# Earlier reciprocals, a one-hot product on VectorE, and tables entered once per three batches, in an attention and mixture-of-experts kernel

## The chip, the cores and the metric

The kernel runs on one core of a Trainium2 chip. The metric is the device time of one execution in microseconds (us). One core has five engines with instruction queues of their own: PE (TensorE, matmuls; PEld is its weight load), DVE (VectorE), ACT (ScalarE), POOL (GpSimd) and SP (SyncE, which here only issues DMAs).

## The reference

Attention over a sliding window, then a mixture of experts on its output:

```
q, k, v: 8 batches x 8 heads x 576 tokens x 64
scores = q k^T / 8 - slope[head] * |i - j|      # only 0 <= i - j < 128
attn   = softmax(scores);  x = attn v           # -> x: 8 x 576 x 512
logits = x w_gate                               # 8 experts
local  = sigmoid(x w_local)
e[s]   = argmax(logits[s]) if s == 0 or local[s] < 0.5 else e[s-1]
out[s] = softmax(logits[s])[e] * (relu(x[s] w1[e]) w2[e])   # F = 1024
```

A token whose local gate is high keeps the expert of the token before it. Each token goes to one expert; how many go to each is known only at run time.

## The kernel before, in words

**Attention, 0 to about 271 us.** 32 slots, one for each batch b and pair of heads p = 0..3, four slots per batch. The order of the operations in a slot is written out by hand in the table ORDER, one string for each p (lines 58 to 63). Each mark is an operation on tokens of the slot: S(i) is the score matmul (i = 0..8, blocks of 64 queries), D(i) the bias and the row minimum on DVE (line 486, the custom operation with the name scs), E(i) the exponential on ACT, which also adds up the row into sm. N3 and N8 normalise: POOL computes r = sm + 1e-9, DVE takes the reciprocal of r, and POOL multiplies the parts by it, parts 0 to 3 in N3 (r of 128x4) and 4 to 8 in N8 (r of 128x5). U(j) are the transposes of the parts on PE into the PSUM tile pt; U0 needs the four parts of N3. C(j) copies pt to SBUF, M(j) multiplies with v, X copies the result and T transposes it on DVE for the store to xd in device memory. A mark with ' belongs to the pair before, and a "." is one step of side work: the gate of the finished batch (route, line 587). All engines' queues are kept in that program order by the class InOrder (line 157), so most of attention's instructions carry line 157 in the profile whatever they do.

**Side work route(b).** It turns the logits of batch b into one-hots (OH, shown as oh_all), the rank of each token at its expert, and from them two one-hot factors: cw (line 671, on POOL; the expert and the block of 32) and RO (line 675, on DVE, shown as ro_all; the row in the block, times the token number val). Five matmuls of RO and cw (pT, in a PSUM tile of the pool ptk, shown as pk) give the token numbers in their places, 0 where there is none. enter (line 687) adds them to the table tbl: z = (ps > 0) * 576 * b in one DVE instruction (tz), and two additions. The numbers in val are those inside one batch, 1 to 576, since the factors are fp16.

**Experts, from about 271 us.** A plan fixed ahead visits each expert with columns of tokens: visit 0 has 256 columns (8 blocks of 32), visit 1 has 384 (299.5 to 337.2 us) and visit 2 has 512 (from 340.1 us); the visits after that are given out by rank at run time. In a visit (Fixed.run, line 973), for eight blocks f of the hidden layer: matmuls h of x and w1, Relu on ACT to hh (line 1001), the low part hl on DVE (line 1002), and matmuls y with w2. Every fp32 product is three matmuls of high and low parts (lines 956 to 958). Weights come by DMA into wraw; split_chunk (lines 230 to 234) casts the high part on ACT and subtracts on DVE for the low part. The rows of x are gathered by POOL (line 172), four tiles t of 128 for a visit of 512; split_x (lines 175 to 182) transposes a tile on DVE (xtr, line 178), casts it on ACT (qx, line 181) and subtracts on DVE (qx, line 182). A visit starts when the qx of all its tiles are there. Operations on nc.vector are placed into DVE's queue by a scheduler; those through InOrder and pin keep their order on each engine.

**Side work of the visits.** During visits 0 and 1 the tables for the visits by rank are made: fill_table (line 841) computes for each batch the one-hots hot (line 848, five DVE instructions, also named cw), five matmuls with ro_all into a pk tile (line 858), and enter into the table trk (128x128). The table then gives the gather indices xidx, ridx and sidx (indices, line 694; fi in the rows). What would be needed for tokens beyond the plan follows (lines 920 to 931: end, efx, off, ge, ef).

Of the kernel before, what the change touches and what calls it, by code (L numbers as in the profile page):

```python
# [8 lines left out]
F32 = mybir.dt.float32  # L9
# [4 lines left out]
ALU = mybir.AluOpType  # L14
AX = mybir.AxisListType
PS = bass.MemoryType.PSUM
P = 128

NB = 8
S = 576  # L20
DM = 512
NE = 8
NT = 5
KS = 4
NS = 3
# [3 lines left out]
NSB = 128  # L29
# [19 lines left out]
def windows(nb):  # L49
# [8 lines left out]
ORDER = [  # L58
# [4 lines left out]
]  # L63
DEPTH = 3
POOL_CUT = 19
PACE = 16
FAR = 1000.0
Z_HOLD = -1.5 * 2.0 ** -23

# [2 lines left out]
def moe_attention(ctx, tc, qT, kT_d, vv, wg, wl, w1, w2, out):  # L72
    nc = tc.nc
    NTOK = NB * S

    cp = ctx.enter_context(tc.tile_pool(name="const", bufs=1))
    st = ctx.enter_context(tc.tile_pool(name="state", bufs=1))
    wr = ctx.enter_context(tc.tile_pool(name="wraw", bufs=RAWS))
    tp = ctx.enter_context(tc.tile_pool(name="tok", bufs=2))

    sh = ctx.enter_context(tc.tile_pool(name="shared", bufs=2))
    ptk = ctx.enter_context(tc.tile_pool(name="ptk", bufs=1, space=PS))
# [16 lines left out]
    own = cp.tile([P, NE], F32, name="own")  # L99
    slots = cp.tile([P, 2, NE], F32, name="slots")  # L100
    rep32 = cp.tile([P, P], F16, name="rep32")
    val = cp.tile([P, NT], F32, name="val")
    msel = cp.tile([P, 4], F32, name="msel")
    quart = cp.tile([P, 4], F32, name="quart")
    roff = cp.tile([P, 1], F32, name="roff")
# [7 lines left out]
    ro_all = st.tile([P, NB, NT, P], F16, name="ro_all")  # L113
# [17 lines left out]
    pin = tc.keep_in_program_order  # L131
# [31 lines left out]
    pe, dve, act, pool = (InOrder(e) for e in (nc.tensor, nc.vector, nc.scalar, nc.gpsimd))  # L163
# [139 lines left out]
    with ExitStack() as actx:  # L303
# [57 lines left out]
        def make_bias(p):  # L361
            o = [bias[64 * h:64 * h + 64, p] for h in range(2)]
            for h in range(2):
                pool.tensor_scalar(o[h], rel[64 * h:64 * h + 64], -8.0 * 2.0 ** -(2 * p + h + 1), 1.0, ALU.mult, ALU.mult)
                yield
            for h in range(2):
                pool.affine_select(o[h], o[h], [[-1, 192]], ALU.is_ge, -8e9, base=128, channel_multiplier=1)
                yield
            for h in range(2):
                pool.affine_select(o[h], o[h], [[1, 192]], ALU.is_gt, -8e9, base=0, channel_multiplier=-1)  # L370
                yield
# [13 lines left out]
        for h in range(2):  # L385
            pool.iota(rel[64 * h:64 * h + 64], [[-1, 192]], base=128, channel_multiplier=1,
                           allow_small_or_imprecise_dtypes=True)
# [13 lines left out]
        def setup():  # L401

            yield from make_bias(2)
            yield from make_bias(3)
            whole = dict(channel_multiplier=0, allow_small_or_imprecise_dtypes=True)
            pool.memset(w32, 0.0)
            nc.sync.dma_start(w32[:, :, 0:8], wg.rearrange("(k p) e -> p k e", p=P))
            nc.sync.dma_start(w32[:, :, 8:9], wl.rearrange("(k p) e -> p k e", p=P))
            yield
            pool.memset(onesb, 1.0)  # L410
            yield
            pool.memset(msel, 1.0)
            yield
            pool.affine_select(utri, onesb, [[1, P]], ALU.is_gt, 0.0, base=0, channel_multiplier=-1)
            yield
            pool.affine_select(msel, msel, [[-32, 4]], ALU.is_ge, 0.0, base=0, channel_multiplier=1)
            yield
            pool.memset(first, 0.0)
            yield
            pool.iota(quart, [[32, 4]], base=0, **whole)  # L420
            yield
            pool.affine_select(msel, msel, [[32, 4]], ALU.is_ge, 0.0, base=31, channel_multiplier=-1)
            yield
            pool.memset(first[0:1, 0:1], 1.0)
            yield
            pool.iota(k8, [[0, NT], [-1, NE]], base=NE, **whole)
            yield
            pool.tensor_tensor(quart, quart, msel, ALU.mult)
            yield
            pool.tensor_copy(identb, ident)  # L430
            yield
            for t in HR:
                pool.memset(t, 0.0)
                yield
            pool.memset(ohs, 0.0)
            pool.memset(g32, 0.0)
            yield
            pool.iota(io16, [[0, NT], [1, 4 * KS]], base=0, **whole)
            yield
            pool.iota(rep32, [[0, 4], [1, 32]], base=0, **whole)  # L440
            yield
            pool.iota(val, [[P, NT]], base=1, channel_multiplier=1, allow_small_or_imprecise_dtypes=True)
            yield
            pool.memset(tbl, 0.0)
            yield
            pool.memset(trk, 0.0)
            yield
            pool.memset(own, 0.0)
            for e, k in enumerate(OWN):
                pool.memset(own[:, e:e + 1], 4.0 * k)  # L450
            yield
            for r in range(NE):
                pool.memset(slots[:, 0, r:r + 1], float(sum(CAP[:r])))
                pool.memset(slots[:, 1, r:r + 1], float(CAP[r]))
                if r % 2:
                    yield
            pool.iota(io32, [[1, NFX]], base=0, **whole)
            yield
            pool.iota(io128, [[1, NSB]], base=1, **whole)
# [127 lines left out]
        def route(b):  # L587
            L = logits_of.pop(b)
            l8 = L[:, :, 0:NE]
            OH, RO = oh_all[:, b], ro_all[:, b]  # L590
# [63 lines left out]
            with nc.allow_low_precision("small whole numbers"):  # L654
# [3 lines left out]
            rf = tp.tile([P, NT], F32, name="rrf")  # L658
# [9 lines left out]
            kh = tp.tile([P, NT, 4 * KS], F16, name="kh")  # L668
            dve.tensor_tensor(kh, io16, k_all[:, b].unsqueeze(2).broadcast_to([P, NT, 4 * KS]), ALU.is_equal)
            cw = tp.tile([P, NT, NSB], F16, name="cw")[:, :, :4 * NS * KS].rearrange("p t (e k) -> p t e k", e=NS)  # L670
            pool.tensor_tensor(cw, OH[:, :, 0:NS].unsqueeze(3).broadcast_to([P, NT, NS, 4 * KS]),
                                   kh.unsqueeze(2).broadcast_to([P, NT, NS, 4 * KS]), ALU.mult)
            yield
            for t in range(NT):
                dve.tensor_scalar(RO[:, t], rep32, rf[:, t:t + 1], val[:, t:t + 1], ALU.is_equal, ALU.mult)
                if t % 2:
                    yield
            yield
# [7 lines left out]

        def enter(table, ps, b):

            z = tp.tile([P, P], F32, name="tz")[:, :table.shape[1]]
            dve.tensor_scalar(z, ps, 0.0, float(S * b), ALU.is_gt, ALU.mult)  # L690
            dve.tensor_tensor(table, table, ps, ALU.add)
            dve.tensor_tensor(table, table, z, ALU.add)

        def indices(t, idx, x0, c0, wins):

# [90 lines left out]
        for slot in range(4 * NB + DEPTH):  # L786
            b, p = divmod(slot, 4)
# [53 lines left out]
    def fill_table(table, fc, pace):  # L841

        fo = {}

        def hot(b):
            fo[b] = tp.tile([P, NT, NSB], F16, name="cw")
            for t in range(NT):
                nc.vector.tensor_scalar(fo[b][:, t], io128, fc[:, b * NT + t:b * NT + t + 1], None, ALU.is_equal)

        hot(0)  # L850
        for b in range(NB):
            for _ in range(pace // 2):
                yield
            if b + 1 < NB:
                hot(b + 1)
            pt = ptk.tile([P, NSB], F32, name="pk")
            for t in range(NT):
                pin(nc.tensor.matmul(pt, ro_all[:, b, t], fo[b][:, t], start=t == 0, stop=t == NT - 1))
            for _ in range(pace - pace // 2):
                yield  # L860
            enter(table, pt, b)

    def rank_tables():

# [26 lines left out]
        nc.vector.tensor_scalar(efx[:, NFX + 1:], er, 0.0, None, ALU.add)  # L891
        nc.vector.tensor_scalar(lo, own, -FAR, None, ALU.add)
        nc.vector.tensor_tensor(hi, lo, cap, ALU.add)
# [6 lines left out]
        kf = tp.tile([P, NA], F32, name="kf", bufs=1)  # L900
        nc.vector.tensor_scalar(kf, ka, -FAR, None, ALU.add)
        nc.vector.tensor_tensor(lo_t, kf, lo_t, ALU.is_ge)
# [3 lines left out]
        nc.vector.scalar_tensor_tensor(a_t, a_t, 1.0, lo_t, ALU.add, ALU.mult)  # L906
        yield
        yield from fill_table(trk, a_t, PACE_TABLE)
        yield from indices(trk, idxs, XO[0], TO[0], [at + w for kind, _, at, nb in PLAN if kind == "rank" for w in windows(nb)])
        rank_done.append(1)  # L910
        for _ in range(PACE):
            yield
# [26 lines left out]
    def beyond_table():  # L939

        nc.vector.memset(tfx, 0.0)
        run(fill_table(tfx, beyond[0], 0))
        run(indices(tfx, idxs, XO[1], TO[1], windows(NSB)))
        nc.sync.dma_start(xidx_d, xidx[:, XO[1]:])
        nc.sync.dma_start(ridx_d, ridx[:, TO[1]:])
        nc.sync.dma_start(sidx_d, sidx[:, TO[1]:])
        nc.sync.dma_start(efx_d, efx[0:1, 0:NFX])
# [297 lines left out]
```

## Time and profile before

| | |
|---|---|
| median of 3 runs | 741.42 us (740.2 to 741.76) |
| profiled execution | 742.23 us, of which its span is 740.5 us |
| mean granted TensorE clock | 0.995 |
| PE busy | 713.2 us (96%) |
| DVE busy | 491.1 us (66%) |
| ACT busy | 431.6 us (58%) |
| POOL busy | 399.8 us (54%) |
| DMA | 121.91 MB, mean 165 GB/s |

The profile is of one execution, by the profiler's clock; a time in it counts from the span's start. A row of the timeline has the start, the busy time, engine, line, operation, out<-in with its shape, the number of equal instructions in a run (x), and in brackets how long the engine was idle before and what released it. A row of a wait table has the total idle time, how often, and the longest. In the table by windows each engine has busy us and, in brackets, instructions; the last three numbers are the granted clock as a share of full speed, DMA's busy share and GB/s.

### The profile page before, as it was taken

To read this page: it belongs to the slowest core of one execution; us is meant where nothing else is said; L and a number is where in the kernel's file an instruction comes from. 1 tells how busy PE (TensorE), PEld (TensorE's weight loads), DVE (VectorE), ACT (ScalarE), POOL (GpSimd) and SP (SyncE) were. 2 spreads that over 40 slices of the span, in tenths; PEclk is the share of its full clock that TensorE was granted. 3 is DMA by queue.
4 is the path that set the end of the run, shared out by engine and by line. 5 is a ranking of instruction groups with operands and counts; after the bars stand their busy time and mean duration, and the time that the engine had idled before them with its cause. 6 is when DMAs were issued, how large, how long until landed. Compare 5 with 4: busy or idle time off the path is not lost. (4 is left out here: it accounts for less than half of the span.)

```text
span 740.5 us, 14838 instructions
## 1 busy us (share of the span) xinstructions
PE 713.2 (96%) x4629; PEld 599.9 (81%) x4629; DVE 491.1 (66%) x1670; ACT 431.6 (58%) x1204; POOL 399.8 (54%) x671
## 2 busy tenths in 40 slices
PE   8899999999999998998999999999999999999996
PEld 5678777777777767886888889889989988888895
DVE  7658686776868799997554366467567557535562
ACT  6778878877877874534343354456456446334553
POOL 6664554545458677577777163744745756402121
PEclk9999999999999999999999999999999999999998
DMA  9966846556372357645445365557558556525560
GB/s 209 199 181 143 195 103 177 157 164 172 104 216 74 87 153 256 194 130 159 139 150 191 93 191 186 169 187 231 176 175 244 179 171 221 162 94 181 164 177 31
DMA packets 94290, 121.91 MB, mean 165 GB/s; under 512 B 46655, under 2 KB 65343, under 8 KB 94208
## 3 DMA queue, kind: packets, MB, share of 16 engines
q1 hardware_dynamic: 83376, 100.26, 46.6%
q0 software_dynamic: 9488, 20.22, 9.2%
q8 instruction: 37, 0.61, 0.3%
q10 hardware_dynamic: 1344, 0.46, 0.3%
q14 instruction: 45, 0.37, 0.2%
HBM read 101.29 MB, written 20.20 MB: 164 GB/s over the span
## 5 line engine op out<-in xcount | busy, mean ns | idle before, releaser
L234 DVE TENSOR_TENSOR cut<-wraw,cut 128x512 fp32r<-128x512 f32 x231 | 152.3, 695 | 53.5 <-ACT cut L232 52.2
L172 POOL DMA_INDIRECT kr<-xd,xidx x141 | 153.2, 1087 | 51.9 <-issue 40.9
L232 ACT CAST cut<-wraw 128x512 fp32r<-128x512 f32 x212 | 120.7, 618 | 58.1 <-PE y L958 57.8
L956 PE MATMUL h<-qx,cut 128*128 128x384 f32 (+6 forms) x440 | 141.7, 322 | 2.9 <-ACT qx L181 2.9
L957 PE MATMUL h<-qx,cut 128*128 128x384 f32 (+6 forms) x440 | 142.0, 323 | 0.5 <-DVE qx L182 0.5
L958 PE MATMUL h<-qx,cut 128*128 128x384 f32 (+6 forms) x440 | 141.7, 322 | 0.0
L157 POOL TENSOR_SCALAR cut<-cut,r 128x192 f32<-128x192 f32 (+2 forms) x256 | 99.6, 407 | 65.6 <-PE pt L157 26.2
L956 PE MATMUL y<-cut,hh 128*128 128x512 f32 x328 | 129.2, 394 | 1.1 <-ACT hh L1001 1.1
L957 PE MATMUL y<-cut,hh 128*128 128x512 f32 x328 | 129.1, 394 | 0.0
L958 PE MATMUL y<-cut,hl 128*128 128x512 f32 x328 | 128.5, 395 | 0.5 <-DVE hl L1002 0.5
L950 POOL DMA_INDIRECT out<-y,sidx x41 | 42.6, 1040 | 155.5 <-ACT y L965 119.9
L1001 ACT ACTIVATE hh<-h 128x384 fp32r<-128x384 f32 (+6 forms) x104 | 47.8, 460 | 128.8 <-PE h L958 128.5
L157 PE MATMUL sc<-kr,qx 128*128 128x192 f32 (+1 forms) x576 | 112.6, 326 | 2.4 <-DVE mn L157 1.7
L157 ACT ACTIVATE cut<-scs,mn 128x192 f32<-128x192 f32 (+2 forms) x256 | 109.7, 431 | 6.1 <-DVE mn L157 4.4
L1002 DVE SCALAR_TENSOR_TENSOR hl<-h,hh 128x384 fp32r<-128x384 f32 (+6 forms) x112 | 56.8, 507 | 84.5 <-ACT hh L1001 82.6
L157 DVE CUSTOM_DVE_ANT_0 scs<-sc,bias 128x192 f32<-128x192 f32 (+2 forms) x288 | 86.7, 326 | 34.8 <-PE sc L157 32.4
L157 PEld LDWEIGHTS sc<-kr,qx 128*128 128x128 f32 x576 | 87.4, 195 | 7.7 <-DVE mn L157 4.7
L956 PEld LDWEIGHTS h<-qx,cut 128*128 128x128 f32 x440 | 83.4, 190 | 10.0 <-ACT qx L181 3.3
L957 PEld LDWEIGHTS h<-qx,cut 128*128 128x128 f32 x440 | 83.5, 190 | 7.3 <-DVE qx L182 0.9
L958 PEld LDWEIGHTS h<-qx,cut 128*128 128x128 f32 x440 | 83.5, 190 | 3.5 <-issue 0.4
L157 PE MATMUL pt<-ident,cut 128*128 128x128 f32 x448 | 72.0, 282 | 6.7 <-POOL cut L157 4.7
L958 PEld LDWEIGHTS y<-cut,hl 128*128 128x128 f32 x328 | 61.5, 188 | 14.8 <-DVE hl L1002 1.9
(223 smaller groups left out, 1042.1 us busy)
## 6 DMA issues: line engine op xcount, KB each, us to landing
wraw<-w SPq DMA_DIRECT2D x120, 512.0 KB
xd<-T SPq DMA_DIRECT2D x8, 1152.0 KB
kr<-kT SPq DMA_DIRECT2D x31, 288.0 KB
qx<-qT SPq DMA_DIRECT2D x61, 144.0 KB
cut<-v SPq DMA_DIRECT2D x8, 1024.0 KB
kr<-xd,xidx POOLq DMA_INDIRECT x141, 3.6
v<-v SPq DMA_DIRECT2D x8, 128.0 KB
out<-y,sidx POOLq DMA_INDIRECT x41, 3.5
```

Source lines behind the costliest of these rows:

```text
L157: ins = getattr(self.engine, name)(*args, **kw)
L172: queued(nc.gpsimd.indirect_dma_start(out=r, out_offset=None, in_=src[0:n, :], in_offset=bass.IndirectOffsetOnAxis(ap=col, axis=0), bounds ...
L232: scalar.copy(c[:, 0, f], raw[:, f])
L234: (pool if 2 * n + f == POOL_CUT else vector).tensor_tensor(c[:, 1, f], raw[:, f], c[:, 0, f], ALU.subtract)
L950: queued(nc.gpsimd.indirect_dma_start(out=out[:, :], out_offset=bass.IndirectOffsetOnAxis(ap=col, axis=0), in_=y, in_offset=None, bounds_c ...
L956: nc.tensor.matmul(o, ah, bh, start=start, stop=False)
L957: nc.tensor.matmul(o, ah, bl, start=False, stop=False)
L958: nc.tensor.matmul(o, al, bh, start=False, stop=stop)
L1001: now.act.activation(hh, hp, AF.Relu)
L1002: nc.vector.scalar_tensor_tensor(hl, hp, 0.0, hh, ALU.max, ALU.subtract)
```

## The change

Four things are changed.

1. ORDER[2] has N3 ahead of D8 where it stood behind it, and ORDER[3] has N3 ahead of D7 where it stood behind D8. The three steps of N3 on POOL, DVE and POOL move together.
2. cw in route is computed on DVE where it was computed on POOL.
3. The token numbers in val run over three batches (GROUP = 3, 1 to 1728), and a batch uses its own third. So enter adds z only for batches 3 to 7, with a base of 1728 or 3456: for batches 0 to 2 it is one addition.
4. fill_table takes one pk tile for a group of three batches, its 15 matmuls (10 in the last group) add up in it, and enter is called once for a group.

```diff
-    "... S6 . D6 . E4 S7 S8 . D7 E5 D8 N3 U2 E6 . X1'",
+    "... S6 . D6 . E4 S7 S8 . D7 E5 N3 D8 U2 E6 . X1'",
-    "... S6 . D6 E4 S7 S8 D7 . E5 D8 N3 T1'' U2 . E6 X1' T0' T1'",
+    "... S6 . D6 E4 S7 S8 N3 D7 . E5 D8 T1'' U2 . E6 X1' T0' T1'",
+GROUP = 3
-    val = cp.tile([P, NT], F32, name="val")
+    val = cp.tile([P, GROUP, NT], F32, name="val")
-            pool.iota(val, [[P, NT]], base=1, channel_multiplier=1, ...)
+            pool.iota(val, [[S, GROUP], [P, NT]], base=1, channel_multiplier=1, ...)
-            pool.tensor_tensor(cw, OH[:, :, 0:NS].unsqueeze(3)...
+            dve.tensor_tensor(cw, OH[:, :, 0:NS].unsqueeze(3)...
-                dve.tensor_scalar(RO[:, t], rep32, rf[:, t:t + 1], val[:, t:t + 1], ALU.is_equal, ALU.mult)
+                dve.tensor_scalar(RO[:, t], rep32, rf[:, t:t + 1], val[:, b % GROUP, t:t + 1], ALU.is_equal, ALU.mult)
         def enter(table, ps, b):
-            z = tp.tile([P, P], F32, name="tz")[:, :table.shape[1]]
-            dve.tensor_scalar(z, ps, 0.0, float(S * b), ALU.is_gt, ALU.mult)
+            base = float(S * (b - b % GROUP))
+            if base:
+                z = tp.tile([P, P], F32, name="tz")[:, :table.shape[1]]
+                dve.tensor_scalar(z, ps, 0.0, base, ALU.is_gt, ALU.mult)
             dve.tensor_tensor(table, table, ps, ALU.add)
-            dve.tensor_tensor(table, table, z, ALU.add)
+            if base:
+                dve.tensor_tensor(table, table, z, ALU.add)
     # in fill_table
-            pt = ptk.tile([P, NSB], F32, name="pk")
+            last = b % GROUP == GROUP - 1 or b == NB - 1
+            if b % GROUP == 0:
+                pt = ptk.tile([P, NSB], F32, name="pk")
             for t in range(NT):
-                pin(nc.tensor.matmul(pt, ro_all[:, b, t], fo[b][:, t], start=t == 0, stop=t == NT - 1))
+                pin(nc.tensor.matmul(pt, ro_all[:, b, t], fo[b][:, t], start=b % GROUP == 0 and t == 0, stop=last and t == NT - 1))
...
-            enter(table, pt, b)
+            if last:
+                enter(table, pt, b)
```

The lines of the kernel after are one higher than before from line 67 on, and up to seven higher in the expert part. How the instructions then stand on the engines, at the three places that matter below:

DVE's queue in the slot p = 3, once per batch, before (ISA rows with scs are the D of the table: D6, D7, D8; the RECIPROCAL is that of N3; rex and oh_all are side work):

```order
L157 TENSOR_TENSOR rex<-L,rm 128x40
L157 ISA scs,mn<-sc,bias 128x192
L157 ISA mn 128x1
L157 ISA scs,mn<-sc,bias 128x192
L157 ISA mn 128x1
L157 TENSOR_TENSOR oh_all<-pk,k_85 128x40
L157 ISA scs,mn<-sc,bias 128x192
L157 ISA mn 128x1
L157 RECIPROCAL r<-r 128x4
L157 STREAM_TRANSPOSE T<-xT 128x6x32
```

And after:

```order
L158 TENSOR_TENSOR rex<-L,rm 128x40
L158 ISA scs,mn<-sc,bias 128x192
L158 ISA mn 128x1
L158 RECIPROCAL r<-r 128x4
L158 ISA scs,mn<-sc,bias 128x192
L158 ISA mn 128x1
L158 TENSOR_TENSOR oh_all<-pk,k_85 128x40
L158 ISA scs,mn<-sc,bias 128x192
L158 ISA mn 128x1
L158 STREAM_TRANSPOSE T<-xT 128x6x32
```

The reciprocal stands between D6 and D7, two D and one small operation sooner.

DVE's queue at the start of the rank tables, during visit 1, before (L848 are the one-hots of hot, L234 the weights' subtractions):

```order
L848 TENSOR_SCALAR cw<-io_88,at_t 128x128 x10
L157 TENSOR_SCALAR tz<-pk 128x128
L157 TENSOR_TENSOR trk<-trk,pk 128x128
L848 TENSOR_SCALAR cw<-io_88,at_t 128x128
L157 TENSOR_TENSOR trk<-trk,tz 128x128
L848 TENSOR_SCALAR cw<-io_88,at_t 128x128 x4
L157 TENSOR_SCALAR tz<-pk 128x128
L157 TENSOR_TENSOR trk<-trk,pk 128x128
L234 TENSOR_TENSOR cut<-wraw,cut 128x512
L157 TENSOR_TENSOR trk<-trk,tz 128x128
```

And after:

```order
L852 TENSOR_SCALAR cw<-io_88,at_t 128x128 x15
L235 TENSOR_TENSOR cut<-wraw,cut 128x512 x2
L852 TENSOR_SCALAR cw<-io_88,at_t 128x128 x5
L158 TENSOR_TENSOR trk<-trk,pk 128x128
L1009 SCALAR_TENSOR_TENSOR hl<-h,hh 128x384
L235 TENSOR_TENSOR cut<-wraw,cut 128x512 x2
```

The first group is entered with one instruction, behind the one-hots of four batches. In the whole stage 7 instructions on trk and tz stand where 24 stood.

DVE's queue at the end of visit 1, before (xtr and qx are of the last tile of visit 2, y is the result of visit 1):

```order
L234 TENSOR_TENSOR cut<-wraw,cut 128x512
L157 TENSOR_SCALAR ridx<-t_5663 128x32
L157 TENSOR_SCALAR iz<-t_5663 128x32
L234 TENSOR_TENSOR cut<-wraw,cut 128x512
L157 SCALAR_TENSOR_TENSOR sidx<-t_5663,iz 128x32
L178 STREAM_TRANSPOSE xtr<-kr 128x512
L234 TENSOR_TENSOR cut<-wraw,cut 128x512
L963 TENSOR_SCALAR y<-y,gs 128x512
L182 TENSOR_TENSOR qx<-xtr,qx 128x4x128
```

And after:

```order
L235 TENSOR_TENSOR cut<-wraw,cut 128x512
L158 TENSOR_SCALAR ridx<-t_5626 128x32
L158 TENSOR_SCALAR iz<-t_5626 128x32
L1009 SCALAR_TENSOR_TENSOR hl<-h,hh 128x384
L158 SCALAR_TENSOR_TENSOR sidx<-t_5626,iz 128x32
L179 STREAM_TRANSPOSE xtr<-kr 128x512
L235 TENSOR_TENSOR cut<-wraw,cut 128x512 x2
L183 TENSOR_TENSOR qx<-xtr,qx 128x4x128
L970 TENSOR_SCALAR y<-y,gs 128x512
```

The last qx now stands ahead of the result y of visit 1, and one hl of visit 1 stands right ahead of the transpose. Between the first one-hots and this transpose stand 17 table instructions and three weight subtractions fewer, and six of the small instructions of lines 920 to 928 more. On ACT the cast of this tile (line 181) now stands ahead of the y of visit 1 and of two weight casts that wait for the end of visit 1; before, it stood behind them.

More of the change, by code (lines that the diff above doesn't have):

```diff
@@ L441, in setup @@
             yield
-            pool.iota(val, [[P, NT]], base=1, channel_multiplier=1, allow_small_or_imprecise_dtypes=True)
+            pool.iota(val, [[S, GROUP], [P, NT]], base=1, channel_multiplier=1, allow_small_or_imprecise_dtypes=True)
             yield
@@ L670, in route @@
             cw = tp.tile([P, NT, NSB], F16, name="cw")[:, :, :4 * NS * KS].rearrange("p t (e k) -> p t e k", e=NS)
-            pool.tensor_tensor(cw, OH[:, :, 0:NS].unsqueeze(3).broadcast_to([P, NT, NS, 4 * KS]),
+            dve.tensor_tensor(cw, OH[:, :, 0:NS].unsqueeze(3).broadcast_to([P, NT, NS, 4 * KS]),
                                    kh.unsqueeze(2).broadcast_to([P, NT, NS, 4 * KS]), ALU.mult)
```

4 rows, old and new, of the table ORDER are left out of this document.

## The prediction

> **What bounds the kernel now.** I read the page's shares first, then the table of waits for PE, then PE's stalls in the timeline.
>
> ```profile
> span 740.5 us, 14838 instructions
> PE 713.2 (96%) x4629; PEld 599.9 (81%) x4629; DVE 491.1 (66%) x1670; ACT 431.6 (58%) x1204; POOL 399.8 (54%) x671
> ```
>
> PE is busy for 96% of the span, so over the whole it is the bound, and the change removes no work that PE needs. It can only move PE's own waits, and those are few. The table of waits (total us, times, longest) has these that the change touches:
>
> ```profile
> PE pt L157 <- POOL cut L157: 4.7, 9, 0.8
> PE h L956 <- ACT qx L181: 2.9, 1, 2.9
> PE pk L157 <- POOL cw L157: 1.9, 1, 1.9
> PE h L957 <- DVE qx L182: 0.5, 1, 0.5
> DVE r L157 <- POOL r L157: 9.9, 15, 1.1
> ```
>
> The first row is U0 of attention waiting for N3's multiplications; the second and fourth are one place, the start of visit 2; the third is the cw of batch 7. Together PE waits 10.0 us here, which caps the gain but for one thing, the clock. The last row is DVE's and matters for a rival.
>
> The start of visit 2, from the timeline:
>
> ```profile
> 336.80 0.39 PE L958 MATMUL y<-cut,hl 128*128 128x512 f32 x1
> 337.23 1.14 ACT L232 CAST cut<-wraw 128x512 fp32r<-128x512 f32 x2 [0.44 <-PE y L958]
> 338.68 0.71 DVE L178 STREAM_TRANSPOSE xtr<-kr 128x512 f32<-128x512 f32 x1
> 339.31 0.66 DVE L234 TENSOR_TENSOR cut<-wraw,cut 128x512 fp32r<-128x512 f32 x1
> 339.42 0.62 ACT L181 CAST qx<-xtr 128x512 fp32r<-128x512 f32 x1 [1.06 <-DVE xtr L178]
> 339.88 0.75 DVE L963 TENSOR_SCALAR y<-y,gs 128x512 f32<-128x512 f32 x1
> 340.09 0.73 PE L956 MATMUL h<-qx,cut 128*128 128x512 f32 x2 [2.90 <-ACT qx L181]
> 340.54 0.69 DVE L182 TENSOR_TENSOR qx<-xtr,qx 128x512 fp32r<-128x512 f32 x1
> 341.28 0.80 PE L957 MATMUL h<-qx,cut 128*128 128x512 f32 x1 [0.45 <-DVE qx L182]
> 344.32 0.39 PE L958 MATMUL h<-qx,cut 128*128 128x512 f32 x1
> 344.55 0.40 PE L956 MATMUL h<-qx,cut 128*128 128x512 f32 x1
> ```
>
> Visit 1 ends on PE at 337.19 (336.80 + 0.39). PE then stands 2.90 us for the cast of the last x tile, which stands behind the transpose of 338.68, and 0.45 us more for its low part, which on DVE stands behind the y of 339.88. The windows say why the transpose is that late (PE, PEld, DVE, ACT, POOL busy; clock, DMA share, GB/s), and a window of PE alone says what the stall leaves behind:
>
> ```profile
> 300.00:330.00 30.00, 29.68 (x177) 25.72 (x175) 29.41 (x120) 11.68 (x22) 21.70 (x20) 1.00 0.55 171
> 330.00:340.00 10.00, 7.19 (x36) 5.96 (x33) 10.00 (x32) 5.58 (x11) 7.66 (x6) 1.00 0.50 159
> ```
>
> ```profile
> 342.00:343.00 1.00, 1.00 (x4) 0.50 0.95 324
> ```
>
> DVE is busy for 29.41 of 30 and 10.00 of 10 us. In this stage DVE, not PE, sets the end: what leaves its queue ahead of the transpose comes off the stall one for one. And after the stall the granted clock is 0.50. From 341.28 to 344.32 stand seven matmuls in 3.04 us; at the 0.23 us from start to start that such a matmul then takes (344.55 - 344.32) they need 1.61. So the stall costs 2.90 + 0.45 + 1.43 = 4.78 us.
>
> **The tables' part.** These rows price what leaves and what comes:
>
> ```profile
> 311.49 1.80 DVE L848 TENSOR_SCALAR cw<-io,at_t 128x128 f16<-128x128 f16 x10
> 325.14 0.29 DVE L157 TENSOR_SCALAR tz<-pk 128x128 f32<-128x128 f32 x1
> 325.34 0.28 DVE L157 TENSOR_TENSOR trk<-trk,pk 128x128 f32<-128x128 f32 x1
> 334.60 0.55 DVE L1002 SCALAR_TENSOR_TENSOR hl<-h,hh 128x384 fp32r<-128x384 f32 x1
> 341.13 0.17 DVE L920 TENSOR_TENSOR_SCAN end<-nf,z 128x8 f32<-128x8 f32 x1
> 342.10 0.41 DVE L930 TENSOR_REDUCE ef<-ge 128x32 f32<-128x256 f32 x1
> ```
>
> From the first one-hot (311.49) to the last transpose (338.68) are 27.19 us, nearly all busy. Seventeen table instructions leave at 0.20 us from start to start (325.34 - 325.14): -3.4. Three subtractions of 128x512 fall behind the transpose; at 0.57 us from start to start (339.88 - 339.31) -1.7. The six small instructions from the scan on come ahead of it: +0.97 (342.10 - 341.13). One hl of visit 1 now stands right ahead of the transpose, and where DVE is earlier it must wait for PE's h there: I allow 0.6, about the busy time of one hl. Sum -3.5: transpose at about 335.2, its cast, 0.74 + 0.62 later, done at 336.5, ahead of PE's 337.19. On ACT the cast no longer stands behind the two weight casts that wait for PE (337.23), so nothing holds it there. The low part follows on DVE after two subtractions, done at about 337.6, and PE needs it two matmuls after 337.19, at 337.65. So the wait is gone or under 0.3, and with it the cause of the half clock. What is late next is the low part, then the hl of block 7, which PE needs about 336 and which comes one or two instructions after 334.60. I take -4.6, between the bounds -4.78 (all gone) and -2.5 (the transpose comes only the 1.7 of the subtractions sooner, since DVE waits for PE's h with what the tables free: the cast is done at 338.3, and a stall of 1.1 + 0.45 and half of the clock's loss, 0.7, stay). The rows of 300 to 340 show DVE without waits, so I stay near the first.
>
> By the Trainium skill, TensorE: Matmul & The Clock Gate, section Part 1: The HAM clock gate, the half clock follows an idle window of about 3.4 us; here 2.90 us of idle time ahead of a window with clock 0.50 is under that figure, so the trace disagrees in size, or the window is not fixed to the gap. If the half clock had another cause and stayed, the 1.43 us would stay too and the sum below would be 6.6 instead of 8.0, 734.9.
>
> The later matmuls of ro_all on PE are the same 40, and their last now stands about ten us of PE work ahead of visit 1's end: nothing. One pk tile held over three batches makes the next group wait for one enter, while PE has weights' matmuls queued behind: the cover is that enter now comes three times, not eight. If it does not hold, PE waits once per group for one 0.28-us addition: 0 to +0.6. The scheduler also issues SP's read of a count (efx) ahead of three weight loads; it waits for an instruction that now comes earlier too: 0 to +0.3, taken 0.
>
> **N3 sooner.** The slot p = 3 of batch 2, and the same wait in the first and the last of seven batches (0 to 6):
>
> ```profile
> 97.02 0.19 POOL L157 TENSOR_SCALAR r<-sm 128x4 f32<-128x4 f32 x1 [2.50 <-ACT cut L157]
> 97.48 0.36 DVE L157 CUSTOM_DVE_ANT_0 scs<-sc,bias 128x192 f32<-128x192 f32 x1
> 98.15 0.17 DVE L157 RECIPROCAL r<-r 128x4 f32<-128x4 f32 x1
> 98.49 1.46 POOL L157 TENSOR_SCALAR cut<-cut,r 128x64 f32<-128x64 f32 x4 [1.28 <-PE pk L157]
> 100.09 0.63 PE L157 MATMUL pt<-ident,cut 128*128 128x128 f32 x4 [0.48 <-POOL cut L157]
> 36.40 0.63 PE L157 MATMUL pt<-ident,cut 128*128 128x128 f32 x4 [0.64 <-POOL cut L157]
> 228.97 0.63 PE L157 MATMUL pt<-ident,cut 128*128 128x128 f32 x4 [0.48 <-POOL cut L157]
> 104.85 0.36 DVE L157 CUSTOM_DVE_ANT_0 scs<-sc,bias 128x192 f32<-128x192 f32 x1 [0.58 <-PE sc L157]
> ```
>
> r is added up at 97.21, but the reciprocal comes at 98.15, behind D7 (97.48) and D8; POOL then needs 1.46 us for four multiplications, and PE stands for 0.48. (The row of 98.49 names PE; pk had long been read, and the reciprocal's end at 98.32 is what came last.) Moved to D7's place, the reciprocal comes 0.67 us sooner, more than the 0.48: the wait goes. D7 and D8 come 0.17 later each; E7 and E8 that follow run into the next slot. Seven such waits are 6 x 0.48 + 0.64 = 3.5 of the 4.7 in the table. Bounds: -1.0, if only 0.15 each comes through because D0 to D2 of the next slot end up bounding it, and -4.7, if the two other waits go with p = 2's move (0.33 us sooner by the same D's duration). I take -3.4: seven times the common 0.48.
>
> The table tbl has six DVE instructions fewer, spread over batches 0 to 2 in a DVE queue that is waiting anyway (104.85): nothing. The wider iota of val is at the start, once: nothing.
>
> **cw on DVE.** No 128x240 product of fp16 runs on DVE before. The rows near it, and the one cw that PE waits for:
>
> ```profile
> 292.17 2.23 DVE L234 TENSOR_TENSOR cut<-wraw,cut 128x512 fp32r<-128x512 f32 x1
> 293.23 0.61 POOL L157 TENSOR_TENSOR cw<-oh_all,kh 128x240 f16<-128x240 f16 x1
> 293.89 0.18 PE L157 MATMUL pk<-cw,ro_all 128*128 128x48 f16 x1 [1.95 <-POOL cw L157]
> 297.23 0.17 PE L866 MATMUL pk<-ohs,onesb 128*128 128x8 f16 x1 [0.41 <-DVE tbl L157]
> 308.51 0.48 DVE L836 TENSOR_TENSOR ge<-oh_all,hi 128x320 f32<-128x320 f16 x1
> ```
>
> The nearest is the product of 128x320 at 308.51: 0.48 x 240 / 320 = 0.36 us. In batches 0 to 6 that is 0.36 more for DVE in a p = 0 slot; the idle 0.58 at 104.85 hides it, and POOL is freed of 0.61. If it does not hide, each batch loses up to 0.36, 7 x 0.36 = 2.5 of the 3.4 above. For batch 7, PE's 1.95 goes, but the RO and cw rows on DVE now come behind more h matmuls on PE, and PE's next stop, at 297.23, is DVE's tbl, so DVE's own chain sets the end: it gains about 0.5 from a subtraction not stretched (2.23 against 0.69) and loses 0.36. Between -0.5 and +0.5 I take 0.
>
> **Sum.** -4.6 - 3.4 = -8.0. The profiled execution took 742.23 us (740.5 its span, 1.7 around it) and would take 734.2. It is 0.8 above the median of 741.42; on the median's basis that is 733.4, and I say 733.5. About 0.2% (1.5 us) is what a measurement of this kernel can tell from no change.
>
> **Rivals.** *The wait at visit 2 goes only in part* (hl of block 7, the low part of x, or the subtractions behind the transpose take its place). For it: DVE stays the bound at 100% in that stage and the cover of the low part is 0.05 us. Against: the cast has 0.7 us to spare. With the bound above, 2.5 instead of 4.6, it gives 735.5; if the whole stall comes back, 738.0.
>
> *Attention gains nothing.* cw stands on DVE while POOL multiplies the parts of N8, and the wider DVE queue delays D0 to D2 by what N3 saves. For it: the row of 292.17, where a DVE subtraction of 0.69 took 2.23 us beside a POOL instruction. Against: the idle 0.58. It gives 741.4 - 4.6 = 736.8. The Trainium skill, SBUF — State Buffer, section SBUF: two separate sides, makes the port that GpSimd and VectorE share a lock which the first to start holds for its whole instruction; the row of 292.17 agrees, and the rule speaks against moving cw to where POOL multiplies.
>
> *Slower.* DVE executes in order, so a reciprocal that stands earlier can wait for POOL's r, with D7 and D8 queued behind it, and E7, E8 and the next slot's parts behind those. In the rows above r is there at 97.21 and the new place is at 97.48, a margin of 0.27; the table has 15 such waits already, the longest 1.1. The 16 moved reciprocals eat the 8.0 at 0.5 us each; at 1.1 on 14 of them, +15.4 - 8.0: 748.8.
>
> *No change:* the whole stall comes back (738.0), and N3's gain is lost but for 1.0 (+2.4): 740.4.
>
> **How the numbers follow.** The forecast 0.55 (its own range 731.5 to 735.5); wait at visit 2 in part 0.17; attention nothing 0.15; no change 0.08; slower 0.05. Faster by over 0.2%: 0.55 + 0.17 + 0.15 = 0.87. Low end of the range: all of PE's 10.0 us above, with the clock's 1.43 and without 1.0 that returns elsewhere, 731.0. High end 738.5 takes in the two partial cases and leaves out no change, slower and their mixtures.
>
> **What would show it.** In the profile after: a RECIPROCAL of 128x4 between two D, and no 0.48 ahead of U0 in the seven slots; 7 instructions on trk and tz at full size; the last xtr of visit 2 about 3.5 us sooner relative to PE's end of visit 1; no wait of PE h for ACT qx and a clock of 1.00 behind it; cw on DVE with about 0.36 us. The prediction is wrong if DVE's waits for POOL's r grow well over 9.9 us, if PE's stall at visit 2 has a new releaser, or if a D row shows over 0.5 us beside cw.

## The result, and the profile after

The kernel after takes 736.12 us (median of 6 runs, 735.18 to 737.31) against 741.59 us before (median of 6, 740.2 to 743.55), a ratio of 0.9916 with a 95% interval of 0.9902 to 0.9929. Forecast were 733.5 us and a range of 731.0 to 738.5. The profiled execution took 735.18 us, its span is 733.5.

The page and PE's waits of the kernel after (its lines are one to seven higher):

```profile
span 733.5 us, 14818 instructions
PE 709.1 (97%) x4629; PEld 596.5 (81%) x4629; DVE 490.2 (67%) x1655; ACT 430.9 (59%) x1204; POOL 392.5 (54%) x663
```

```profile
PE pt L158 <- ACT pts L158: 4.4, 9, 0.6
PE y L963 <- ACT hh L158: 1.6, 1, 1.6
PE pt L158 <- POOL cut L158: 0.8, 1, 0.8
PE pk L158 <- DVE ro_all L158: 0.6, 1, 0.6
DVE r L158 <- POOL r L158: 10.1, 17, 1.1
```

PE's wait of 2.9 and 0.5 us for qx is gone. The nine waits of pt are still there: 4.4 and 0.8 us instead of 4.7 and 0.6, now put down to ACT's copy and not to POOL. The wait for cw is gone too, and 1.6 and 0.6 us of other waits stand in the same place. DVE's waits for POOL's r hardly grew.

The start of visit 2, timeline and windows of the kernel after:

```profile
333.21 0.71 DVE L179 STREAM_TRANSPOSE xtr<-kr 128x512 f32<-128x512 f32 x1
333.95 0.62 ACT L182 CAST qx<-xtr 128x512 fp32r<-128x512 f32 x1 [0.85 <-DVE xtr L179]
335.01 0.69 DVE L183 TENSOR_TENSOR qx<-xtr,qx 128x512 fp32r<-128x512 f32 x1
335.45 0.62 PE L963 MATMUL h<-qx,cut 128*128 128x512 f32 x2
```

```profile
300.00:330.00 30.00, 29.90 (x172) 24.79 (x171) 28.45 (x115) 10.73 (x22) 23.09 (x22) 1.00 0.55 176
330.00:340.00 10.00, 10.00 (x48) 8.45 (x47) 9.71 (x28) 5.99 (x11) 7.75 (x7) 1.00 0.55 173
335.00:345.00 10.00, 10.00 (x46) 8.26 (x45) 7.53 (x17) 4.74 (x9) 7.87 (x8) 1.00 0.60 195
```

PE starts visit 2 at 335.45 with no idle time ahead. The transpose stands 2.24 us ahead of that point, where before it stood 1.49 us behind the end of visit 1: 3.7 us sooner, for 3.5 forecast. The cast is done at 334.57, 0.88 ahead, and the low part at 335.70, about when PE comes to it. The clock stays at 1.00 behind it too (335 to 345), where before it fell to 0.50 from 341 on.

By positions on PE the 6.9 us between the two profiled executions divide so. Up to the first transpose of attention: 12.99 before and 11.31 after, -1.7, which the last section takes for chance. From there to the U0 of batch 6 (228.97 and 226.26): -1.0. From there to the routing's last matmul (297.23 and 294.91): +0.4. These two, -0.6, are all that N3, cw and the table tbl bring. From there to the start of visit 2 (340.09 and 335.45): -2.3. From there to the last matmul (732.90 and 725.99): -2.3. The last two, 4.6, are the tables' part; the profile with that part alone, below, has -2.3 and -2.2 there (295.39, 335.95 and 726.57). Without the start -5.2 remain, and the medians say -5.5.

### The profile page after: what moved, and what is told of

Its sections match the earlier page's. It is cut to its first block, busy times and chain, and to the rows that moved or that the text cites. A ratio compares the mean times of both kernels' runs of the same rounds, so it can differ in the third digit from the quotient of the medians.

```text
span 733.5 us, 14818 instructions
## 1 busy us (share of the span) xinstructions
PE 709.1 (97%) x4629; PEld 596.5 (81%) x4629; DVE 490.2 (67%) x1655; ACT 430.9 (59%) x1204; POOL 392.5 (54%) x663
## 5 line engine op out<-in xcount | busy, mean ns | idle before, releaser
L235 DVE TENSOR_TENSOR cut<-wraw,cut 128x512 fp32r<-128x512 f32 x231 | 150.4, 688 | 53.6 <-ACT cut L233 52.3
L158 PE MATMUL sc<-kr,qx 128*128 128x192 f32 (+1 forms) x576 | 111.0, 322 | 2.8 <-DVE mn L158 1.3
L158 PEld LDWEIGHTS sc<-kr,qx 128*128 128x128 f32 x576 | 85.5, 191 | 8.1 <-DVE mn L158 5.2
```

The lines of the kernel that those rows point to most:

```text
L158: ins = getattr(self.engine, name)(*args, **kw)
L235: (pool if 2 * n + f == POOL_CUT else vector).tensor_tensor(c[:, 1, f], raw[:, f], c[:, 0, f], ALU.subtract)
```

## The experiments

All times in this section stand beside runs of the kernel before on the same chip, whose median was 742.74 us in the first four and 742.38 in the others.

**The tables' part alone**: ORDER and cw of before, the rest of after.

```diff
 # the kernel after, but
-    "... S7 S8 . D7 E5 N3 D8 U2 ..."          # p = 2
+    "... S7 S8 . D7 E5 D8 N3 U2 ..."
-    "... S7 S8 N3 D7 . E5 D8 T1'' U2 ..."     # p = 3
+    "... S7 S8 D7 . E5 D8 N3 T1'' U2 ..."
-            dve.tensor_tensor(cw, OH ...
+            pool.tensor_tensor(cw, OH ...
```

> The kernel after with ORDER as before and cw on POOL as before: token numbers over three batches and one entry per group alone. Theory (the tables' part is the gain): the wait of PE for the last x tile at the start of visit 2 and the half clock behind it go, 4.6 us, so 741.6 - 4.6 = 737.0; the seven waits of 0.48 us at U0 stay, and the 1.9 us for cw of batch 7 stay. Rival (N3 or cw bring part of it): 738.5 or more.

737.2 us, ratio 0.9927 (0.9910 to 0.9943). The whole change has 0.9916, inside this interval. PE's waits:

```profile
PE pt L158 <- POOL cut L158: 4.7, 9, 0.9
PE pk L158 <- POOL cw L158: 1.9, 1, 1.9
```

Attention's and batch 7's waits stand as before, and the wait at visit 2 is gone. So this part is the gain, as far as it can be measured.

**N3 sooner alone**: the kernel before with the two strings of ORDER from after.

> The kernel before with N3 sooner in ORDER alone. Theory (U0 is held twice, by POOL's parts and by ACT's copy of the pt tile before, both ending at 99.95 in the trace of before): the seven waits keep their 0.48 us and are put down to ACT's copy; 0 to -0.5 us, 741.1 to 741.6. Rival (the prediction: N3 sooner frees PE, and cw on DVE is what takes it back in the whole change): -3.4, 738.2.

742.5 us, ratio 0.9994 (0.9976 to 1.0012).

```profile
PE pt L157 <- ACT pts L157: 4.4, 9, 0.6
PE h L956 <- ACT qx L181: 2.9, 1, 2.9
```

The nine waits are those of the kernel after, with ACT's copy as the releaser. The prediction's -3.4 is excluded; -0.9, which the trace allows (from U0 to U0 a batch takes 99.63 - 67.74 = 31.89 us, before 100.09 - 68.09 = 32.00, and there are eight), is not.

**cw on DVE alone**: the kernel before with `dve` for `pool` in that line.

> The kernel before with cw on DVE alone. Theory: nothing in batches 0 to 6, since PE's waits there are not DVE's, and 0 to -0.5 us in batch 7: 741.1 to 741.6. Rival (cw on DVE delays attention's D and takes back N3's gain): +2.5, 744.1.

743.17 us, ratio 1.001 (0.9999 to 1.0021): no gain, and no loss of 2.5 us. The rival by which cw on DVE eats N3's gain falls: N3 alone had no such gain, and a batch takes 101.20 - 69.20 = 32.00 us here, as before.

**Where attention's gain is held.** N3's multiplications ended at 98.49 + 1.46 = 99.95 in the kernel before. This is ACT's queue there at the same place, which the prediction didn't show:

```profile
98.94 0.45 ACT L157 ACTIVATE cut<-scs,mn 128x192 f32<-128x192 f32 x1
99.39 0.56 ACT L157 COPY pts<-pt 128x512 f32<-128x512 f32 x1
```

The copy of the pair before, C2', ends at 99.95 as well. pt has two buffers, so U0 needs the one that C2' frees as much as it needs N3's parts. In the kernel after only one of the two has moved:

```profile
95.25 0.16 DVE L158 RECIPROCAL r<-r 128x4 f32<-128x4 f32 x1
95.58 1.48 POOL L158 TENSOR_SCALAR cut<-cut,r 128x64 f32<-128x64 f32 x4 [0.57 <-PE sc L158]
97.18 0.56 ACT L158 COPY pts<-pt 128x512 f32<-128x512 f32 x1
97.88 0.63 PE L158 MATMUL pt<-ident,cut 128*128 128x128 f32 x4 [0.48 <-ACT pts L158]
```

POOL is done at 97.06, 0.68 us ahead of the copy's end at 97.74, and PE still waits its 0.48. In ORDER[0] the copy stands behind the exponential E7'; the next three runs change places there.

**After, with the copy first:**

```diff
-    "U3' S0 S1 . S2 E7' C2' D0 D1 U0 E8' ..."
+    "U3' S0 S1 . S2 C2' E7' D0 D1 U0 E8' ..."
```

> The kernel after with C2' ahead of E7' in ORDER[0], so that ACT copies the pt tile of the pair before one exponential (0.63 us) sooner. Theory (the copy is what U0 now waits for): the seven waits of 0.48 us go, up to -3.4 against after: 732.7 to 734, less what E7' and N8' lose by being 0.46 us later. Rival (something else holds U0 at the same time again, or N8' becomes late): 736.1 or slower.

736.17 us, ratio 0.9916 (0.9897 to 0.9935), the same as after.

```profile
97.18 0.63 PE L158 MATMUL pt<-ident,cut 128*128 128x128 f32 x4
98.18 0.59 PE L158 MATMUL sc<-kr,qx 128*128 128x192 f32 x2 [0.37 <-DVE mn L158]
```

U0 starts without a wait, so the copy was what held it. One step later PE stands 0.37 us at S3, which needs a score tile that D0 frees, and D0 is behind five small operations of the routing on DVE. From U0 to U0 a batch takes 31.9 us, as in the kernel after. The expected 732.7 to 734 was wrong; the rival, that something else binds, was right.

**Before, with the copy first** (the same edit to the kernel before):

> The kernel before with C2' ahead of E7' in ORDER[0], N3 not moved. Theory (two binders that end together): U0 keeps its wait of about 0.48 us, now put to POOL's parts alone, in the slots p = 0. Rival (ACT's copy alone was the binder, POOL only named): the waits go without N3 being moved.

One run, 744.85 us; only the trace tells here.

```profile
67.50 0.69 PE L157 MATMUL pt<-ident,cut 128*128 128x128 f32 x4
68.51 0.76 PE L157 MATMUL sc<-kr,qx 128*128 128x192 f32 x3 [0.32 <-DVE mn L157]
```

```profile
66.33 1.47 POOL L157 TENSOR_SCALAR cut<-cut,r 128x64 f32<-128x64 f32 x4 [1.28 <-PE pk L157]
67.47 0.52 PEld L157 LDWEIGHTS pt<-ident,cut 128*128 128x128 f32 x4 [0.31 <-POOL cut L157]
```

My expectation was wrong: without N3's move six of the seven waits of U0 go too. U0's four transposes take the four parts one by one, and PE starts the first at 67.50, though POOL's four multiplications end only at 66.33 + 1.47 = 67.80. The 0.31 us ahead of the weight load are not POOL's, though the row names it. In the kernel after with the copy first, POOL ended at 95.31 + 1.48 = 96.79, and the row has nearly the same idle time and the same name:

```profile
97.15 0.42 PEld L158 LDWEIGHTS pt<-ident,cut 128*128 128x128 f32 x4 [0.30 <-POOL cut L158]
```

What POOL costs here is the stretch of the four transposes, 0.69 us against 0.63. So ACT's copy held the start of U0 in the kernel before, and POOL, which the profile named, did not. The batch is no shorter for it: 99.51 - 67.50 = 32.01 us from U0 to U0, since PE now waits 0.32 us at S3.

**After, with the copy first and the routing step later:**

```diff
-    "U3' S0 S1 . S2 E7' C2' D0 D1 U0 E8' ..."
+    "U3' S0 S1 S2 C2' E7' D0 D1 U0 . E8' ..."
```

> The kernel after with C2' ahead of E7' and the step of side work that stood ahead of D0 now behind U0, both in ORDER[0]. In the run with C2' alone the wait of PE at U0 was gone, and 0.37 us of it came back at S3, which waits for D0 to free a score tile; D0 stood on DVE behind five small side-work operations (97.32 to 97.90). Theory (a chain of binders, each 0 to 0.5 us behind the one before): D0 comes 0.58 sooner and the 0.37 goes; in the trace six slots p = 0 get 0.37 shorter, 2.2 to 2.6 us, 733.5 to 734. Rival (the next binder, N8' or E0, stands as close again): 0 to 1 us, 735 to 736.1.

735.93 us, ratio 0.9909 (0.9888 to 0.9929).

```profile
68.41 0.59 PE L158 MATMUL sc<-kr,qx 128*128 128x192 f32 x2 [0.19 <-DVE mn L158]
100.14 0.59 PE L158 MATMUL sc<-kr,qx 128*128 128x192 f32 x2 [0.19 <-DVE mn L158]
```

A third binder stands there, again DVE's, at 0.19. A batch takes 31.73 us (100.14 - 68.41), after 97.88 - 66.00 = 31.88, before 32.00. By the trace this is 1.1 us over seven batches better than after; the interval doesn't tell the two apart, so it is not shown to be a better version.

**One for one, and the clock.** In the kernel after, the last transpose of visit 2's x is done once more, or three times more, with the same result; each brings weight subtractions ahead of it in DVE's queue.

```diff
-        pin(nc.vector.transpose(t, r.rearrange("p q c -> p (q c)")))
+        for _ in range(1 + again):
+            pin(nc.vector.transpose(t, r.rearrange("p q c -> p (q c)")))
```

Once more:

> The kernel after with the last transpose of visit 2's x done once more on DVE (same result). Theory (DVE sets this end one for one once its slack is used): the transpose and a subtraction between put the last xtr 1.2 us later, against a slack of 0.88 of the cast; PE waits about 0.3 for the cast and 0.5 to 0.9 for the low part, which now stands behind y; the clock stays at 1.00, since the stall is short. Rival (another slack hides it): no wait.

```profile
335.05 0.69 DVE L180 STREAM_TRANSPOSE xtr<-kr 128x512 f32<-128x512 f32 x1
336.45 0.73 PE L965 MATMUL h<-qx,cut 128*128 128x512 f32 x2 [0.29 <-ACT qx L183]
337.63 0.50 PE L966 MATMUL h<-qx,cut 128*128 128x512 f32 x1 [0.45 <-DVE qx L184]
```

```profile
337.00:338.00 1.00, 0.55 (x3) 1.00 0.73 115
```

The transpose comes 1.2 us later than the first (333.85), the slack of 0.88 is used up, and PE waits 0.29 and 0.45 with the clock at 1.00: as expected. The one run took 738.78 us, with a stretch of half clock at another place, about 610 us (last section).

Three times more:

> The kernel after with the last transpose of visit 2's x done three times more on DVE (same result). Theory: three transposes and three subtractions put the last xtr 3.6 us later, PE waits about 2.7 for the cast, as in the kernel before, and the granted clock falls to 0.50 behind it for about 3 us; the time is that of before in this stage. Rival (the half clock was not the stall's doing): same wait, clock 1.00.

```profile
337.59 0.71 DVE L180 STREAM_TRANSPOSE xtr<-kr 128x512 f32<-128x512 f32 x1
339.00 0.93 PE L965 MATMUL h<-qx,cut 128*128 128x512 f32 x2 [2.70 <-ACT qx L183]
340.19 0.79 PE L966 MATMUL h<-qx,cut 128*128 128x512 f32 x1 [0.25 <-DVE qx L184]
```

```profile
341.00:342.00 1.00, 1.00 (x3) 0.50 0.79 291
```

The stall of the kernel before is back, 2.70 and 0.25 us for 2.90 and 0.45, and the half clock with it; the one run took 742.45 us. So DVE's queue ahead of this transpose sets the start of visit 2, and the stall brings the half clock.

## Why the prediction was right or wrong

The measured 736.12 lies inside the stated range, 731.0 to 738.5, but outside the forecast's own, 731.5 to 735.5: of its two gains one came and one did not.

**The tables' part: right, its exact size in part by luck.** Forecast were -4.6 us, and the positions on PE give -4.6. The steps agree too: seven instructions on trk and tz where 24 were, the transpose 3.7 us sooner against PE, no new releaser at visit 2. Two sizes inside it were off and cancel. The half clock cost 1.71 us and not 1.43 (its first part lay in the two matmuls ahead of 341.28), so the place had 5.06 us to give. And visit 1 itself takes 0.5 us longer after: first h to first h of visit 2 is 40.40 before, of which 2.90 is the stall, and 38.02 after.

The term that was put at nothing here is "The later matmuls of ro_all on PE are the same 40". They are the same 40, but among the large matmuls of visit 1 they stand in 21 groups, where before they stood in 10, most of them of five. A large matmul with such a group behind it takes 0.27 us from start to start, and one without 0.17 (kernel after):

```profile
300.33 0.33 PE L965 MATMUL h<-qx,cut 128*128 128x384 f32 x1
300.50 0.33 PE L963 MATMUL h<-qx,cut 128*128 128x384 f32 x1
310.36 0.42 PE L964 MATMUL h<-qx,cut 128*128 128x384 f32 x1
310.63 0.23 PE L864 MATMUL pk<-cw,ro_all 128*128 128x128 f16 x1
```

Eleven more groups at that price are about 1 us, an estimate from these rows, and cover the 0.5. All six profiles with the tables' part have 21 groups and 38.0 to 38.3 us for visit 1 without its stall, and all four without it have 10 groups and 37.3 to 37.5 us. No run changed the groups alone, so this cause is read from the traces and not shown by an experiment.

**N3: wrong, by 2.4 us, most of what the forecast missed by.** The step that failed is "Moved to D7's place, the reciprocal comes 0.67 us sooner, more than the 0.48: the wait goes." The reciprocal came sooner as said, and POOL too, but PE's wait was for ACT's copy, which ended in the same hundredth of a microsecond as POOL's last multiplication, and the profile names only one. Instead of -3.4 the trace has -1.0 up to the U0 of batch 6, where the wait still stands:

```profile
226.26 0.63 PE L158 MATMUL pt<-ident,cut 128*128 128x128 f32 x4 [0.48 <-ACT pts L158]
```

That is the smaller of the bounds that the prediction gave, though it gave another reason (D0 to D2 of the next slot). The run with N3 alone has -0.9 up to the same place. The rival "attention gains nothing", 736.8 with a chance of 0.15, came nearest to 736.12, but for another reason than it gave: cw on DVE took 0.53 us in attention, not 0.36, and the run with cw alone showed no change of a batch's length. By the Trainium skill, SBUF — State Buffer, section SBUF: two separate sides, the lock between GpSimd and VectorE spoke for that rival; a DVE subtraction of 0.69 beside POOL's did take 2.23 us before, yet the lock is not what held attention.

**cw of batch 7: inside the forecast's -0.5 to +0.5, but a small loss and not zero.** PE's 1.95 us went, and this came in its place (kernel after):

```profile
290.23 0.50 PE L963 MATMUL y<-cut,hh 128*128 128x512 f32 x1 [1.56 <-ACT hh L158]
292.13 0.40 DVE L158 TENSOR_TENSOR cw<-oh_all,kh 128x240 f16<-128x240 f16 x1
294.30 0.20 PE L158 MATMUL pk<-cw,ro_all 128*128 128x48 f16 x1 [0.62 <-DVE ro_all L158]
```

The two waits, 1.56 and 0.62, are 0.2 us more than the one. From the U0 of batch 6 to the routing's last matmul PE takes 68.7 us after and 68.3 before. In the six profiles with cw on DVE it is 68.7 to 69.4 us, in the four with cw on POOL 68.0 to 68.6, without the 1.70 us of half clock that two of these have. With N3's 2.4 this 0.4 makes up the 2.8 us by which this part of the forecast was off.

**The slower rival: no.** DVE waits for POOL's r 17 times and 10.1 us in all, for 15 and 9.9 before. The margin at the new place held: in the slot shown above POOL's r ends 0.25 us ahead of the reciprocal at 95.25, for 0.27 forecast. No D row is longer than 0.36 us, beside cw or elsewhere, where 0.5 was named as a sign.

## What to carry to other kernels

A wait is released by the last of its holders, and the profile names one, not always the right one: before a gain is booked, look up when every other operand and the buffer that the waiting instruction writes to came free, and take the distance to the second as the gain at that place. Here that was one row of ACT's queue. Where PE is near full, ordering by hand meets a chain of binders 0.2 to 0.5 us apart, and each removed one gives at most the step to the next. Work taken out of the queue that is busy for 100% of a stage came off the stall one for one, and took the slow clock with it.

## What the runs showed of the hardware that I had not expected

The half clock is partly chance. In all profiles of this study a stretch of it while PE has work costs 1.70 to 1.71 us, which at clock 0.50 is 3.4 us long. The stall of 2.7 to 2.9 us at visit 2 brought one in each of the five profiles that had it. The waits of 1.1 and 0.5 us about 610 us, which every kernel here has, brought one in five of ten profiles. One stood at 20 to 25 us in two of the ten, and one at 292 to 298 in two of the four that have the wait of 1.9 us for cw. This is the one about 610 of the run with one more transpose:

```profile
607.00:609.00 2.00, 1.51 (x5) 0.74 0.16 49
609.00:611.00 2.00, 2.00 (x10) 0.50 0.45 127
611.00:613.00 2.00, 2.00 (x12) 0.90 0.93 285
```

2 x (0.26 + 0.50 + 0.10) is 1.7 us. So runs of one kernel differ by such stretches, and the time of one run says little about 1 us. By the Trainium skill, TensorE: Matmul & The Clock Gate, section Part 1: The HAM clock gate, the gate looks at a free-running window of about 3.4 us; the length of a stretch agrees with that, but waits of 1.1 and 0.5 us were enough in half of the cases, far under an idle window.

The start shows the same, without the clock's column showing it. Kernel before, then after:

```profile
5.24 2.47 PE L157 MATMUL sc<-kr,qx 128*128 128x128 f32 x8 [0.59 <-DMA qx<-qT]
```

```profile
5.16 1.01 PE L158 MATMUL sc<-kr,qx 128*128 128x128 f32 x6 [0.68 <-DMA qx<-qT]
```

These matmuls take 0.31 us each in the one and 0.17 in the other on average, and the first six alone 1.30 and 0.68 us from the first start to the last, with a clock of 1.00 in both tables of windows. The other runs show all of it: eight in 2.47 us with N3 alone and with the copy first in the kernel before, and 2.02 in the run with copy and step; the fast speed is there with the tables alone (eight in 1.54) and with cw alone, a kernel without the tables' part (six in 1.01). So the speed changes at another moment each time, and the 1.7 us at the start are taken for chance. Something of that size does vary within one kernel: spans of the kernel before with the same mean clock, 0.995, go from 738.9 to 741.0 us on one chip. But the start was slow in three of the four profiles without the tables' part and only in one of the six with it, so a share of the change in it is not excluded; several profiles of one and the same kernel would settle it, and were not taken.
